# Top-32 attention and gated FFN on one core: the 64-row tiles of two head pairs worked as one couple, with three q, k and v buffers

## The chip, the core and the metric

The kernel runs on one core of a Trainium2 chip. The metric is the device time of one launch in microseconds (us). All operands are float32 in HBM. TensorE is called PE here, VectorE DVE, ScalarE ACT, GpSimd POOL and the engine that issues all loads and stores SP.

## The reference, cut to what matters

```python
def _attn_ref(q, k, v):                      # each (8, 8, 576, 64)
    scores = matmul(q, k.transpose(0, 1, 3, 2)) / sqrt(64)
    kth = np.partition(scores, -32, axis=-1)[..., -32:-31]
    scores = np.where(scores >= kth, scores, -1e9)
    attn = exp(scores - max(scores))
    attn = attn / (sum(attn) + 1e-09)
    return matmul(attn, v)

def _moe_ref(x, w_in, conv_w, w_out):        # x (8, 576, 512), d_ff 1024, 3 taps
    h = np.maximum(x @ w_in, 0.0)
    conv_out = sum over k of conv_w[k] * h shifted by k - 1 along the sequence
    return (h * sigmoid(conv_out)) @ w_out
```

## The kernel before, in words

Heads are worked in pairs: 8 batches of 4 pairs, and a pair's two heads lie on the two halves of the 128 partitions of q and k. The 576 query rows are four blocks of 128 and one of 64. A batch is worked in two parts (`PARTS`): part 0 has blocks 0 to 2 of all four pairs, part 1 has block 3 and the block of 64 rows (`None`). One tile of work is 128 partitions of 576 scores. A block of 128 rows gives two tiles, one per head (`t.h` 0 and 1). The block of 64 rows gives one tile, a *single*, with head 1 on the lower 64 partitions and head 0 on the upper. A batch so has 24 tiles in part 0 and 12 in part 1, in all 288. In part 1 the order is head 0, head 1, single, for each pair in turn.

A function `iteration(it)` writes out, tile by tile, what PE, DVE, ACT and POOL do in a fixed order. Several tiles are in flight: the tile that gets its scores in an iteration is 7 ahead of the one that DVE weighs, and that is one ahead of the one that PE transposes. The steps:

- `fetch` (L210) loads k (704 columns, 352 KB) and q (576 columns, 288 KB) of a pair on SP, one piece ahead; `nat` has two buffers (`NATB`). `load_v` (L215) loads v, in the iteration in which the pair's first tile reaches the stage `tC`.
- `edge_product` (L221) and `scores` (L227) fill the PSUM banks `s_ps[0]`, `s_ps[1]` and the 128 columns `edge_ps`, with the last 64 key columns of both heads. For a block of 128 rows both heads' scores are made at once, at `t.h == 0` (L242); a single has two products of 64 rows by 64 columns of the array (L235) for 512 keys and two for 64 keys.
- `evacuate` (L244, ACT) copies the scores to SBUF; DVE finds candidates for the 32nd largest (L266, L286, L288); ACT makes the signs (L300); POOL multiplies (L305); DVE takes a maximum (L315) and selects the threshold (`select`, L319); ACT makes the exponentials (`expo`, L312) into one PSUM buffer; DVE masks, weighs and sums (`weigh`, L333).
- `transposes` (L338, PE) and `transposed` (ACT) turn the weights; `tails` (L355, PE) and `tailed` (L360, ACT) do so for the last 64 columns. For a single, `tailed` is two copies of 64 by 64 (L367). `av` (L369, PE) multiplies with v; `av_out` (L383, ACT) copies the result out.
- An iteration is `crowded` (L795) when it makes the scores of an ordinary block; an `av` that would fall in a crowded iteration is put off to the next one.
- Between these PE works off pieces of the FFN (`Expand` L454, `Contract` L611), so many per iteration as a written budget gives: `FEED` 1.65 in part 0, `LEAN` 1.3 in part 1. Their other steps are on ACT (relu L468, tanh L515), POOL and DVE (gate L523).
- `inverses` (DVE) and `norms` (PE, ACT, then SP: one store of the sums and eight or more loads that spread them, `rb`) follow when two pairs are done.
- In the first iterations the weights, which come as float64, are converted, block by block (`Convert`, DVE L163, L164 and L175, ACT L168 to L172, POOL).
- After the last tile a loop works off what is left of the FFN. That loop stands outside the written order, and a planner may place its work earlier.

## Time and profile before

| | us |
|---|---|
| time before, median of 3 runs | 1126.01 (1123.76 to 1126.7) |
| the profiled execution | 1126.22 |
| its span | 1124.3 |
| busy PE / DVE / ACT / POOL | 1041.0 / 1044.5 / 985.1 / 959.8 |
| mean granted PE clock, share of full | 0.986 |

The profile shows one execution. Busy is the time in which an engine had an instruction running; PE's ends are modelled, and a busy PE is not always PE at its peak. Idle time of an engine is put down to what released it.

### The profile page before, as it was taken

The page shows a single profiled execution, that of the slowest core. Times are in us where ns is not written, and L with a number is a line of the kernel's source. Part 1 is how long each engine was busy: PE and PEld are TensorE (multiplying, and loading weights), DVE is VectorE, ACT ScalarE, POOL GpSimd, SP SyncE. Part 2 cuts the span into 40 slices and gives each one's busy share as a digit, 9 for nine tenths or more (in the row PEclk, how much of TensorE's full clock was granted, in tenths as well). Part 3 has the DMA queues.
Part 4 walks back from the last instruction along what each step waited for, and adds up shares of the span by engine and source line. Part 5 has one row for each costly group of instructions (what it writes and reads, how often), then busy time and mean ns, then how long its engine had stood idle before and what let it go on. Part 6 is the DMA issues. An engine that isn't in the chain of part 4 may idle for free.

```text
span 1124.3 us, 28000 instructions
## 1 busy us (share of the span) xinstructions
PE 1041.0 (93%) x7970; PEld 766.5 (68%) x7970; DVE 1044.5 (93%) x5822; ACT 985.1 (88%) x2504; POOL 959.8 (85%) x1260
## 2 busy tenths in 40 slices
PE   6765589999999999999999999999999999999997
PEld 1443356676777777776777777776777777776885
DVE  6999999999999999999999999999999999999760
ACT  6999989999899998989989898989989898989641
POOL 5989979799898989899898999899898999899800
PEclk9989889999999999999999999999999999999999
DMA  7232231123221331223221321223221331222101
GB/s 254 89 101 79 68 100 56 61 75 115 74 78 51 119 100 54 71 74 123 73 71 60 119 99 54 70 74 126 70 74 60 115 97 60 69 72 82 27 27 44
DMA packets 71157, 92.28 MB, mean 82 GB/s; under 512 B 12848, under 2 KB 37712, under 8 KB 70992
## 3 DMA queue, kind: packets, MB, share of 16 engines
q1 hardware_dynamic: 70992, 90.38, 25.1%
q8 instruction: 66, 1.08, 0.4%
q14 instruction: 99, 0.81, 0.2%
HBM read 80.76 MB, written 9.58 MB: 80 GB/s over the span
## 4 chain that ended last, share of the span: by engine, by line
PE 72%; DVE 17%; ACT 8%; issue 1%; DMA 1%; SPq 0%; ACTq 0%
PE mc L611 15%; PE me L454 14%; PE pt L345 11%; PE mixed L377 11%; PE s L242 9%; DVE cand L266 4%; DVE e L333 3%; DVE z L315 3%; PE mixed L380 2%; PE s L235 2%; PE mixed L225 2%; ACT weights_ps L312 2%; PE mixed L358 2%; PE weights_ps L611 1%; ACT side L300 1%
## 5 line engine op out<-in xcount | busy, mean ns | idle before, releaser
L266 DVE MAX8 cand<-rows 128x8 f32<-128x82 f32 (+1 forms) x2016 | 483.9, 242 | 0.0
L305 POOL TENSOR_TENSOR z<-rows,side 128x579 f32<-128x579 f32 x288 | 347.3, 1206 | 58.5 <-ACT side L300 56.2
L333 DVE SCALAR_TENSOR_TENSOR e<-rows,kth,weights_ps 128x576 f32<-128x576 f32 x288 | 232.2, 806 | 1.5 <-PE mixed L358 0.9
L454 PE MATMUL me<-x_hi,wi 128*128 128x258 f32 (+1 forms) x952 | 229.9, 312 | 1.0 <-ACT g L468 1.0
L312 ACT ACTIVATE weights_ps<-rows,z 128x576 f32<-128x576 f32 x288 | 219.9, 764 | 6.1 <-DVE e L333 4.4
L300 ACT ACTIVATE side<-rows 128x576 bf16<-128x576 f32 x288 | 222.9, 774 | 0.0
L315 DVE MAX8 z<-z 128x8 f32<-128x576 f32 x288 | 214.3, 744 | 1.8 <-POOL z L305 1.8
L345 PEld LDWEIGHTS pt<-ident,e 128*128 128x128 f32 x1152 | 124.5, 144 | 121.5 <-issue 47.6
L611 PE MATMUL mc<-wo,split 128*128 128x512 f32 x732 | 197.1, 402 | 0.0
L353 ACT COPY pT<-pt 128x512 f32<-128x512 f32 x256 | 152.5, 596 | 49.0 <-PE pt L345 48.0
L345 PE MATMUL pt<-ident,e 128*128 128x128 f32 x1152 | 193.6, 292 | 0.2 <-DVE e L333 0.2
L242 PE MATMUL s<-k,q 64*128 64x512 f32 x512 | 178.3, 671 | 3.7 <-ACT rows L248 3.6
L248 ACT COPY rows<-s 128x512 f32<-128x512 f32 x288 | 166.6, 578 | 16.2 <-PE s L242 13.2
L377 PE MATMUL mixed<-pT,vn 128*64 128x128 f32 (+1 forms) x2560 | 166.1, 273 | 2.1 <-ACT pTt L363 2.1
L454 PEld LDWEIGHTS me<-x_hi,wi 128*128 128x128 f32 x952 | 162.9, 191 | 1.7 <-ACT g L468 1.7
L377 PEld LDWEIGHTS mixed<-pT,vn 128*64 128x64 f32 x2560 | 130.7, 139 | 24.1 <-issue 7.2
L611 PEld LDWEIGHTS mc<-wo,split 128*128 128x128 f32 x732 | 128.9, 189 | 20.5 <-issue 0.2
L454 PE MATMUL me<-x_lo,wi 128*128 128x258 f32 (+1 forms) x476 | 142.0, 298 | 0.0
L487 POOL TENSOR_SCALAR t<-g,cr 128x256 f32<-128x256 f32 (+1 forms) x230 | 117.4, 511 | 0.0
L286 DVE MAX8 rows<-cand 128x8 f32<-128x21 f32 x576 | 107.0, 186 | 0.0
L501 POOL TENSOR_TENSOR t<-t,t 128x256 f32<-128x256 f32 (+1 forms) x115 | 92.3, 803 | 9.6
L454 PEld LDWEIGHTS me<-x_lo,wi 128*128 128x128 f32 x476 | 91.1, 191 | 0.0
(133 smaller groups left out, 1788.0 us busy)
## 6 DMA issues: line engine op xcount, KB each, us to landing
k<-in_k_dram SPq DMA_DIRECT2D x64, 352.0 KB
q<-in_q_dram SPq DMA_DIRECT2D x64, 288.0 KB
vn<-in_v_main_dram SPq DMA_DIRECT2D x64, 256.0 KB
out_dram<-o SPq DMA_DIRECT2D x26, 256.0 KB
rb<-row SPq DMA_DIRECT2D x64, 96.0 KB
raw<-in_w_in_dram SPq DMA_DIRECT2D x16, 256.0 KB
vt<-in_v_tail_dram SPq DMA_DIRECT2D x64, 64.0 KB
raw<-in_w_out_dram SPq DMA_DIRECT2D x16, 256.0 KB
```

What stands on the lines that cost most here:

```text
L242: nc.tensor.matmul(s_ps[h], lhsT=qx[d, at], rhs=kx[d, h * TAIL:h * TAIL + MAIN], start=True, stop=True)
L248: nc.scalar.copy(out=x[:, at:at + MAIN], in_=s_ps[t.h])
L266: yield lambda c=c, at=at, n=n: nc.vector.max(out=t.cand[:, c:8 * CHUNKS:CHUNKS], in_=t.x[:, at:at + n])
L300: nc.scalar.activation(out=t.side[:, 2:S + 2], in_=t.x, func=AF.Sign, scale=-OVER, bias=t.row[:, 7:8], accum_out=t.cnt)
L305: nc.gpsimd.tensor_tensor(t.z[:, 8:S + 11], t.row[:, 6:S + 9], t.side, ALU.mult)
L312: nc.scalar.activation(out=e_ps, in_=t.x, func=AF.Exp, scale=scale, bias=t.shift)
L315: nc.vector.max(out=t.z[:, 0:8], in_=t.z[:, 10:S + 10])
L333: nc.vector.scalar_tensor_tensor(out=t.e, in0=t.x, scalar=kth[:, t.n:t.n + 1], in1=e_ps, op0=ALU.is_ge, op1=ALU.mult, accum_out=t.pc.sums[ ...
L345: nc.tensor.transpose(tp[:, i * P:(i + 1) * P], t.e[:, o + i * P:o + (i + 1) * P], ident)
L377: nc.tensor.matmul(a[r, 0:w], lhsT=st.pc.vn[:, h, i], rhs=st.pT[:, 1 - h if st.single else h, i, 0:w], start=(i == 0), stop=False)
L454: nc.tensor.matmul(mm[:, 0:w], lhsT=wt, rhs=xx, start=(n == 0), stop=(n == len(ops) - 1))
L611: nc.tensor.matmul(mm[0:m], lhsT=x[:, i], rhs=wo[:, e, f], start=start, stop=stop)
```

## The change

The blocks of 64 rows of two pairs (an even one and the odd one after it) become one *couple* of two tiles, which is treated like an ordinary block of two tiles: the even pair's 64-row block is tile `t.h == 0` and goes to bank `s_ps[0]`, the odd pair's is `t.h == 1` and goes to `s_ps[1]`. In the even pair's tile head 1 is on the lower partitions, in the odd pair's tile head 0 is. The number of tiles stays 288. In part 1 the order becomes two tiles of the even pair, two of the odd pair, two of the couple, so all iterations alternate between crowded and not.

Per couple: four products of 64 by 64 quarters of the array for 512 keys, and two products of the whole array for 64 keys each, from padded operands that the host lays out (`last` behind q, `both` behind k); one evacuation of 128 edge columns at `t.h == 0`; one tail transposition; four tail copies of 64 by 64; the `av` of both pairs one after another, from one weights tile. `fetch` loads only the q columns that the part needs (384 or 320 instead of 576; k 704 or 768), into three buffers; it may run six tiles ahead. `load_v` is three stages later (`tE`), with three buffers. At the start one pair is fetched ahead of the first weights, not two.

```diff
-NATB = 2
+NATB = 3
+VB = 3
+AHEAD = 6
...
     def fetch(pc):
-        for nm, src in (("k", k), ("q", q)):
-            x = pc.nat[nm] = nat.tile([P, src.shape[3]], F32, name=nm, bufs=NATB)
-            nc.sync.dma_start(out=x, in_=src[pc.b, pc.g])
+        last = None in PARTS[pc.part]
+        for nm, src, a, z, w in (("k", k, 0, S + 3 * TAIL if last else S + 2 * TAIL, S + 3 * TAIL),
+                                 ("q", q, pc.c0, S + P if last else pc.c1, WIDE)):
+            x = pc.nat[nm] = nat.tile([P, w], F32, name=nm, bufs=NATB)
+            nc.sync.dma_start(out=x[:, 0:z - a], in_=src[pc.b, pc.g, :, a:z])
...
     def edge_product(t):
         t.edged = True
-        row = row_of(t.st.i)
-        at = slice(row, row + P)
-        nc.tensor.matmul(edge_ps, lhsT=t.pc.nat["q"][:, at], rhs=t.pc.nat["k"][:, S:S + 2 * TAIL], start=True, stop=True)
+        if t.single:
+            for one in (t, t.mate):
+                nc.tensor.matmul(edge_ps[:, one.h * TAIL:(one.h + 1) * TAIL],
+                                 lhsT=one.pc.nat["q"][:, one.st.c + TAIL:one.st.c + TAIL + P],
+                                 rhs=one.pc.nat["k"][:, S + 2 * TAIL:S + 3 * TAIL], start=True, stop=True)
...
     def scores(t):
...
+        for one in (t, t.mate) if t.single else (t,):
+            kx, qx, at = one.pc.nat["k"], one.pc.nat["q"], one.st.c
+            for h in range(2):
+                d, keys = slice(h * D, (h + 1) * D), slice(h * TAIL, h * TAIL + MAIN)
+                if t.single:
+                    r = slice(half_of(one, h) * D, (half_of(one, h) + 1) * D)
+                    nc.tensor.matmul(s_ps[one.h][r], lhsT=qx[d, at:at + TAIL], rhs=kx[d, keys], start=True, stop=True)
...
     def evacuate(t):
...
-        if t.single:
-            nc.scalar.copy(out=x[:, MAIN:S], in_=edge_ps[:, 0:TAIL])
-        elif t.h == 0:
+        if t.h == 0:
...
     def tailed(t):
...
+        for one in (t.mate, t):
+            c = slice(one.h * TAIL, (one.h + 1) * TAIL)
             for h in range(2):
-                r = slice(h * TAIL, (h + 1) * TAIL)
-                nc.scalar.copy(out=pTt[r, 0:TAIL], in_=t.tp[0:TAIL, (1 - h) * TAIL:(2 - h) * TAIL])
+                at = half_of(one, h) * TAIL
+                nc.scalar.copy(out=pTt[h * TAIL:(h + 1) * TAIL, c], in_=tail_ps[c, at:at + TAIL])
...
-        crowded = n < NT and not work[n].single and work[n].h == 0
+        crowded = n < NT and work[n].h == 0
...
-            if t.k == 0 and n and pcs.index(pc) + 1 < len(pcs):
-                fetch(pcs[pcs.index(pc) + 1])
+            tiles[n] = work[n]
+            while state.fetched < len(pcs) and n >= pcs[state.fetched].first - AHEAD and (
+                    state.fetched < NATB or n > pcs[state.fetched - NATB].scored):
+                fetch(pcs[state.fetched])
+                state.fetched += 1
...
-        if tC is not None and tC.k == 0:
-            load_v(tC.pc)
+        if tE is not None and tE.k == 0:
+            load_v(tE.pc)
...
             if both:
                 tail_next.append(tE)
-                tE.st.at = it + 1
-                av_next.append(tE.st)
+                for st in tE.unit.sts:
+                    st.at = it + 1
+                    av_next.append(st)
...
-        for pc in pcs[0:2]:
-            fetch(pc)
+        fetch(pcs[0])
+        state.fetched = 1
         load_blocks(W_FIRST)
```

## Rows read from the trace of the kernel before

**Rows 1.** The page: busy us of each engine, share of the span, instructions.

```profile
PE 1041.0 (93%) x7970; PEld 766.5 (68%) x7970; DVE 1044.5 (93%) x5822; ACT 985.1 (88%) x2504; POOL 959.8 (85%) x1260
```

**Rows 2.** One line, the weighing on DVE: min/median/max ns, first and last start.

```profile
L333 DVE SCALAR_TENSOR_TENSOR e<-rows,kth,weights_ps x288: 792/806/817, 27.9 to 1051.7; 128x576 f32<-128x576 f32 x144
```

**Rows 3.** Windows, parts 0 and 1 of batches 3, 4: length, engines, PE clock, DMA.

```profile
422.18:507.65 85.47, 85.15 (x658) 64.55 (x658) 81.56 (x470) 77.04 (x194) 78.43 (x104) 1.00 0.23 72
507.65:549.90 42.25, 38.36 (x341) 27.77 (x340) 41.24 (x239) 39.51 (x103) 37.62 (x49) 1.00 0.34 106
549.90:632.79 82.89, 82.69 (x646) 63.32 (x645) 81.25 (x470) 76.73 (x194) 76.23 (x99) 1.00 0.22 70
632.79:675.46 42.67, 41.18 (x356) 30.40 (x353) 41.39 (x239) 39.18 (x103) 39.84 (x50) 1.00 0.33 106
```

**Rows 4.** Timeline of DVE: start, us, instruction, idle time before it and releaser.

```profile
137.55 0.23 DVE L319 SCALAR_TENSOR_TENSOR hot<-weights_ps,cnt,z 128x10 f32<-128x10 f32 x1 [0.26 <-ACT weights_ps L312]
...
429.29 0.23 DVE L319 SCALAR_TENSOR_TENSOR hot<-weights_ps,cnt,z 128x10 f32<-128x10 f32 x1 [0.69 <-ACT weights_ps L312]
...
1051.33 0.23 DVE L319 SCALAR_TENSOR_TENSOR hot<-weights_ps,cnt,z 128x10 f32<-128x10 f32 x1 [2.08 <-ACT weights_ps L312]
```

**Rows 5.** Timeline of ACT ahead of the wait that ends at 429.29.

```profile
427.43 0.59 ACT L353 COPY pT<-pt 128x512 f32<-128x512 f32 x1 [0.67 <-PE pt L345]
427.91 0.42 ACT L367 COPY pTt<-mixed 64x64 f32<-64x64 f32 x2
428.34 0.27 ACT L387 COPY xt<-mixed 128x128 f32<-128x128 f32 x1
428.50 0.75 ACT L312 ACTIVATE weights_ps<-rows,z 128x576 f32<-128x576 f32 x1
```

**Rows 6.** Timeline of PE: scores of a single, then of an ordinary block.

```profile
503.13 1.08 PE L235 MATMUL s<-k,q 64*64 64x512 f32 x4
...
504.04 0.28 PE L235 MATMUL mixed<-k,q 64*64 64x64 f32 x4
...
506.89 1.13 PE L242 MATMUL s<-k,q 64*128 64x512 f32 x4
```

**Rows 7.** One group by form: shapes, count, busy us, mean ns, idle before.

```profile
L358 PE MATMUL mixed<-ident,e 128*64 128x128 f32 x32 | 9.2, 287 | 12.2 <-ACT pTt L363 8.3 <-ACT xt L387 4.0
```

**Rows 8.** Timeline of PE: products with v of a block, then of a single.

```profile
417.48 1.09 PE L377 MATMUL mixed<-pT,vn 128*64 128x128 f32 x16
418.40 0.39 PE L380 MATMUL mixed<-pTt,vt 128*64 128x128 f32 x4
418.62 0.63 PE L377 MATMUL mixed<-pT,vn 128*64 128x64 f32 x16
419.08 0.29 PE L380 MATMUL mixed<-pTt,vt 128*64 128x64 f32 x4
```

**Rows 9.** Timeline of the start: SP, PE, DVE and ACT, with idle times.

```profile
1.65 0.43 SPq L213 DMA_DIRECT2D k<-in_k_dram  x1
...
2.60 0.43 SPq L153 DMA_DIRECT2D raw<-in_conv_w_dram  x1
...
4.68 0.77 PE L225 MATMUL mixed<-k,q 128*128 128x128 f32 x2 [4.68 <-DMA q<-in_q_dram]
7.67 0.19 DVE L163 TENSOR_SCALAR mc<-raw 128x24 uint32<-128x24 uint32 x1 [5.60 <-DMA raw<-in_conv_w_dram]
...
8.84 0.58 ACT L248 COPY rows<-s 128x512 f32<-128x512 f32 x1
```

**Rows 10.** Timeline of SP: the last of eight spreading loads, and a load of v.

```profile
409.82 0.61 SPq L414 DMA_DIRECT2D rb<-row  x1
411.37 0.35 SPq L218 DMA_DIRECT2D vn<-in_v_main_dram  x1
```

**Rows 11.** Windows behind that load of v: the last two columns are DMA share and GB/s.

```profile
414.00:415.00 1.00, 1.00 (x6) 0.30 (x4) 1.00 (x11) 0.37 (x2) 0.92 (x3) 1.00 0.00 0
```

**Rows 12.** The chain that ended last, in order of time, at the end.

```profile
1110.59 5.48 PE weights_ps L611 x24
```

More of the change, by code (lines that the diff above doesn't have):

```diff
@@ L73, in attend_and_feed @@
     v_main, v_tail = v
-    B, NPAIR, _, S = q.shape
+    (B, NPAIR), S = q.shape[:2], out.shape[1]
     D = P // 2
@@ new lines, in scores @@
+    def scores(t):
+        if t.h:
+            return
+        if not t.edged:
+            edge_product(t)
+        for one in (t, t.mate) if t.single else (t,):
[5 more added lines that the diff above has]
+                    nc.tensor.matmul(s_ps[one.h][r], lhsT=qx[d, at:at + TAIL], rhs=kx[d, keys], start=True, stop=True)
+                else:
+                    nc.tensor.matmul(s_ps[h], lhsT=qx[d, at:at + P], rhs=kx[d, keys], start=True, stop=True)
@@ L681, in attend_and_feed, with add_unit @@
     pcs, work = [], []
+    def add_unit(sts):
+        unit, pair = Box(), []
+        for h in range(2):
+            st = sts[h % len(sts)]
+            t = Box()
+            t.n, t.k, t.h, t.pc, t.st, t.single, t.unit = len(work), st.pc.n, h, st.pc, st, len(sts) > 1, unit
+            t.edged = False
+            st.pc.n += 1
+            st.pc.scored = len(work) - h
+            work.append(t)
+            pair.append(t)
+        unit.sts = sts
+        pair[0].mate, pair[1].mate = pair[1], pair[0]
+        for h, st in enumerate(sts):
+            st.unit, st.off = unit, h * TAIL
+            st.half = [half_of(pair[h], i) for i in range(2)] if len(sts) > 1 else range(2)
     for b in range(B):
@@ L685, in attend_and_feed @@
                 pc = Box()
[L686 to L689 removed]
+                pc.b, pc.g, pc.part, pc.nat, pc.n, pc.sts = b, g, part, {}, 0, []
+                pc.c0 = pc.c1 = MAIN if blocks[0] is None else blocks[0] * P
                 for i in blocks:
                     st = Box()
[L692 to L701 removed]
+                    st.pc, st.c, st.w, st.final = pc, pc.c1 - pc.c0, TAIL if i is None else P, i == blocks[-1]
+                    pc.c1 += st.w
+                    pc.sts.append(st)
+                pcs.append(pc)
+                pc.first = len(work)
+                for st in pc.sts:
+                    if st.w == P:
+                        add_unit([st])
+                if g % 2 and None in blocks:
+                    add_unit([x.sts[blocks.index(None)] for x in pcs[-2:]])
     NT = len(work)
@@ L794, in iteration @@
             pass
-        crowded = n < NT and not work[n].single and work[n].h == 0
+        crowded = n < NT and work[n].h == 0
         avs = [st for st in av_next if not crowded or it > st.at]
         av_next = [st for st in av_next if st not in avs]
-        both = tE is not None and tE.ends
+        both = tE is not None and tE.h == 1
         if tE is not None:
@@ L873, in iteration @@
         while recs and not crowded:
-            norms(recs.pop(0), s_ps[1 if n < NT and work[n].single else 0])
+            norms(recs.pop(0), s_ps[0])
         rec_next = recs + rec_next
@@ L877, in iteration @@
             tails(tE)
-        if n + 1 < NT and not (work[n].single or work[n + 1].single or work[n + 1].h):
+        if n + 1 < NT and not work[n + 1].h:
             edge_product(work[n + 1])
@@ L933 @@
     nc = tc.nc
-    B, NPAIR, _, S = q.shape
+    (B, NPAIR), S = q.shape[:2], out.shape[1]
     DM, DF = w_in.shape
@@ L1001, in _layout @@
     ends = ends.reshape(B, H // 2, 2 * D, -1)
+    both = np.concatenate([k[:, h::2, main:].transpose(0, 1, 3, 2) for h in range(2)], axis=2)
+    last = np.zeros((B, H // 2, 2, D, 2, S - main), q.dtype)
+    for h in range(2):
+        for g in range(H // 2):
+            last[:, g, h, :, h if g % 2 else 1 - h] = q[:, 2 * g + h, main:].transpose(0, 2, 1)
+    last = last.reshape(B, H // 2, 2 * D, -1)
     tails = np.zeros((B, H // 2, 2, S - main, 2, D), v.dtype)
@@ L1006, in _layout @@
     arrays = {
-        "q": pairs(q, lambda h: False),
-        "k": np.concatenate([pairs(k, lambda h: h % 2 == 1), ends], axis=-1),
+        "q": np.concatenate([pairs(q, lambda h: False), last], axis=-1),
+        "k": np.concatenate([pairs(k, lambda h: h % 2 == 1), ends, both], axis=-1),
         "v_main": v[:, :, :main].reshape(B, H // 2, 2, main // P, P, D).transpose(0, 1, 4, 2, 3, 5),
```

80 lines of the change are left out of this document (25 added, 55 removed).

## The prediction

> **What bounds the kernel now.** I read the page first, then the weighing line, then windows, then the timelines around single waits. The page says little by itself: PE and DVE are both busy for 93% of the span [rows 1]. The weighing line gives the clockwork: 288 weighings from 27.9 to 1051.7 us, 3.57 us apart on average [rows 2]. So the span is a start of 28 us, 1024 us of tiles, and 72 us in which the rest of the FFN is worked off.
>
> Cut at the weighings, the windows show who fills the tile phase [rows 3]. In part 1 DVE is busy for 41.24 of 42.25 us (batch 3) and 41.39 of 42.67 (batch 4), while PE is at 38.36 and 41.18. In part 0 PE is busy for nearly all of it (85.15 of 85.47, 82.69 of 82.89) and DVE for 81.56 and 81.25. So DVE's work, which the change leaves as it is, is a floor. In part 1 only about 1 us in 42 lies above it, and the part in which PE is full is the one whose work does not change. That is the main argument against a large gain.
>
> What lies above the floor are short waits on DVE. Its timeline shows waits whose line is mostly the selection L319, released by ACT [rows 4]. Sorted by the tile that is weighed next, 29 of them, 16.4 us, fall in part 1 or on the first four tiles after one (the first, at 137.55 us, and the last, 2.08 us at 1051.33, are shown). Six of these, 4.4 us, are in the last part 1, where the pipeline drains; the other 23 hold 12.0 us. From batch 1 on another 26 waits, 11.5 us, lie deep in part 0 and stay. One wait shows the mechanism: ahead of 429.29 ACT had waited 0.67 us for PE's transpositions, then made the two tail copies of a single, 0.42 us, a copy of 0.27 us, and only then the exponentials for which DVE stood 0.69 us [rows 4, 5]. PE's lateness and ACT's copies add up.
>
> **The change, part by part.** The sum is made against the profiled execution, 1126.22 us (span 1124.3 and 1.9 around it), which is 0.2 us above the median of 1126.01.
>
> *The start.* Today conv_w is queued behind two pairs' k and q, 2 x (352 + 288) = 1280 KB; then behind one pair's, 352 + 192 = 544 KB. SP issues it two places earlier, 2.60 - 1.65 = 0.95 us, and 736 KB less lie ahead. Two loads of 640 KB each, issued from 0.74 and 1.65 us, have let the first q through at 4.68 and conv_w at 7.67 [rows 9], so about 640 KB cost at most 3 us. DVE waited 5.60 us for conv_w, and the first evacuation on ACT, at 8.84, stands behind its conversion. The scores are ready sooner than that, since PE begins them at 4.68 us. I take 1.5 us earlier, between 0 (a later weight block is what holds, for the second pair's loads now stand between the blocks) and 2.2 us.
>
> *PE's work.* Two singles cost 2 x (1.08 + 0.28) = 2.7 us of scores [rows 6]. A couple has four products for 512 keys. If all four quarters run together they cost what one single's two do, 1.08 us; if not, twice that, 2.16. The nearest rows speak for the first: the two quarters of a single take 1.08 us and the two halves of an ordinary block, with twice the columns, 1.13 [rows 6], so products in separate parts of the array run side by side. I take 1.08. The two edge products I put at the 0.28 us of a single's four, the nearest row. Together 1.36, with one tail transposition of 0.29 us less [rows 7]: 1.6 us saved per couple (bounds 0.5 and 1.6), 16 couples, 26 us of PE (8 to 26). The products with v keep their number. Today a single's can fall into one iteration with an ordinary block's, 1.09 + 0.39 + 0.63 + 0.29 [rows 8]; then a couple's two fall together, 2 x (0.63 + 0.29) = 1.84, so the heaviest iteration gets 0.56 us lighter.
>
> A rule of the Trainium skill speaks against the side by side: TensorEngine Tiling (Array Packing), under Gotcha 1: PSUM Pressure, says that different row tiles cannot access the same PSUM bank simultaneously. A single's two products are in different row halves and write one bank, and their 1.08 us is no longer than the 1.13 us into two banks [rows 6], so here the trace differs from the rule. By the rule a couple's scores would take the 2.16 us, and the time would be that of the third rival.
>
> *What PE's saving is worth.* Only waits above the floor can go: the 12.0 us, if each of them is PE's doing. In the wait that I traced, 0.67 us was PE's and 0.42 us the tail copies'. I take half, 6.0 us, bounds 0 and 12.0.
>
> *ACT's copies.* The couple makes four tail copies in one iteration where a single made two: 0.42 us more at a place where expo had no room left [rows 5]. In the sum over six tiles nothing is added, and one copy of 128 edge columns replaces two of 64. ACT has room on average (39.51 of 42.25 us [rows 3]), so only the bunching can cost: 16 x 0.42 = 6.7 us if all of it shows, 0 if PE's earliness covers it. I take half of it, 3.2 us.
>
> *Loads.* Less traffic, on nobody's path: the DMA share is 0.22 to 0.34 [rows 3], and after the first q no wait of PE names k, q or v. Three buffers let SP run ahead; nothing waits for that today, so 0. The later load of v costs cover: its lead falls from six iterations to three, 10.5 us. SP spends 8 x 0.61 = 4.9 us on eight spreading loads that can stand ahead of such a load, and v itself, issued from 411.37, has landed by 414, since the queue then moves nothing [rows 10, 11]: 4.9 + 2.6 = 7.5 us, under the 10.5, so hidden by 3.0 us. Without that cover PE would stand in `av`, with its transpositions queued behind. In part 1 a fetch of k and q may now wait for the couple's scores; v and the sums are behind it on SP, with the same three iterations of lead. No new wait stands on DVE.
>
> *The end.* The last couple's products with v and copies come later by one single's, 0.92 + 0.42 us, but the chain from there to 1116 is PE on FFN products [rows 12], which fill that gap. I take 0; if the cover fails 1.3 us more, and if the drain's longest wait goes 2.1 us less [rows 4].
>
> Sum: -1.5 - 6.0 + 3.2 = -4.3, so 1126.2 - 4.3 = **1121.9 us**. With all good ends it would be 1109.9 (-2.2 - 12.0 - 2.1), with all bad ones 1134.2 (+6.7 + 1.3).
>
> **The rivals.**
>
> *Nothing but the start.* DVE's floor takes PE's saving and ACT's bunching is just covered: 1126.2 - 1.5 = 1124.7. For it: 97 to 98% busy DVE in part 1. Against: the waits at 429.29 and its like begin with PE.
>
> *All waits go.* PE's 1.6 us per couple keeps it ahead of ACT throughout, the copies are covered: 1126.2 - 1.5 - 12.0 - 2.1 = 1110.6. Against: half of a traced wait is not PE's.
>
> *The quarters don't run together*, so the change does not do what it says: 0.5 of 1.6 us is saved, 6.0 x 0.5 / 1.6 = 1.9 us of waits go, the copies cost their 3.2: 1126.2 - 1.5 - 1.9 + 3.2 = 1126.0.
>
> *ACT becomes the late one*, and the kernel slower. Place: the crowded iteration after a couple's transposition, where signs, evacuation, transposed copy, four tail copies and a result copy all stand ahead of expo. Price 0.42 us a couple, 6.7 in all, with no wait gone: 1126.2 - 1.5 + 6.7 = 1131.4. It decides from the point at which expo has under 0.42 us of room before the selection; at 429.29 it had none [rows 4, 5]. Against: PE's transpositions may come earlier. The Trainium skill says the like, in TensorEngine Tiling (Array Packing), PSUM Bottleneck: tiling speeds up TensorE but not PSUM evacuation, and the copy may become the bottleneck. No run here shows it yet.
>
> A late v would cost about 1 us at 16 ends of two pairs, some 1141; the 3.0 us of cover speak against it.
>
> **How the numbers follow.** About 0.3%, 3.4 us, can be told from no change here: faster means under 1122.8, slower over 1129.6. Chances: the forecast 0.40 (its own range 1118 to 1124, a quarter of it above 1122.8), only the start 0.22, all waits 0.11, quarters in turn 0.08, ACT late 0.16, v late 0.03. Faster: 0.30 + 0.11 + 0.04 = 0.45; slower 0.15 + 0.03 + 0.02 from the edges of others = 0.20; the same 0.35. The range reaches to all waits gone and to ACT late, 1111 to 1131.5, with half of each beyond it and v late: 0.16 left out.
>
> **What would show it.** Start: the first weighing at 26.4 instead of 27.9 us. Quarters: eight records in about 1.1 us for a couple; about 2.2 would prove the third rival. Waits: in part 1 and just behind it about 6 us of DVE's idle time fewer, and new ones of up to 0.4 us behind four tail copies. PE's busy time in a part 1 stretch falls by some 3 us while DVE's stays at 41.2 to 41.4. A PE wait that names v would show the load too late. The prediction is wrong if the part 0 stretches change by more than 1 us, for nothing in my sum acts there, or if the stretch after 1052 us differs by over 2 us, which the planner's freedom there allows.

## The result, and the profile of the changed kernel

The changed kernel takes 1114.69 us (median of 4 runs, 1114.14 to 1115.66), the kernel before 1125.43 in the same comparison. The ratio is 0.9906, with a 95% interval of 0.9889 to 0.9924: faster by 10.7 us where 4.3 were forecast. The direction was right and the time lies inside the range; the size is two and a half times the forecast.

The profiled execution of the changed kernel took 1114.14 us, with a span of 1112.0. Its page, busy us of each engine, share of the span and instructions, against [rows 1]:

```profile
PE 1023.4 (92%) x7890; PEld 760.7 (68%) x7890; DVE 1042.2 (94%) x5824; ACT 978.7 (88%) x2483; POOL 955.2 (86%) x1257
```

The weighing line, with min/median/max ns and the first and last start, against [rows 2]:

```profile
L337 DVE SCALAR_TENSOR_TENSOR e<-rows,kth,weights_ps x288: 791/803/816, 25.6 to 1042.0; 128x576 f32<-128x576 f32 x144
```

So the start became 2.4 us shorter (27.9 to 25.55), the tiles 7.3 us (1023.75 to 1016.45), and what follows the last weighing 2.6 us (72.6 to 70.0). The windows of parts 0 and 1 of batches 3 and 4, with the columns of [rows 3]:

```profile
416.78:501.67 84.89, 84.89 (x677) 65.33 (x676) 81.45 (x470) 76.67 (x196) 79.41 (x106) 1.00 0.23 70
501.67:543.11 41.44, 39.83 (x325) 29.13 (x323) 41.07 (x238) 38.24 (x99) 38.40 (x50) 1.00 0.30 93
543.11:626.38 83.27, 79.93 (x650) 60.75 (x649) 81.05 (x471) 77.28 (x196) 75.60 (x98) 1.00 0.21 68
626.38:668.15 41.77, 40.15 (x328) 29.46 (x326) 41.13 (x239) 38.14 (x98) 38.27 (x49) 1.00 0.30 92
```

Part 1 fell from 42.25 and 42.67 us to 41.44 and 41.77. Part 0 fell by 0.58 us in batch 3 and rose by 0.38 in batch 4. Over all batches part 0 gave 2.2 us, part 1 5.1; of the latter 1.5 are in batch 0 alone, a stretch that differs by as much between the variants of the changed kernel below that have three buffers (40.9 to 42.6 us). DVE's busy time fell as well, by 0.1 to 0.3 us a stretch in this table, though the same instructions ran.

What DVE waited for, us in total, times, longest:

```profile
DVE hot L323 <- ACT weights_ps L519: 16.3, 40, 0.7
DVE hot L323 <- ACT weights_ps L316: 7.2, 11, 2.7
```

By the tile that is weighed next, 12 waits of 7.9 us lie in part 1 or on the four tiles behind it (29 of 16.4 us before), and 40 of 15.9 us deep in part 0 (26 of 11.5 before). Many short ones, released by the tanh on ACT, have taken the place of fewer long ones. Six of the forty, of 0.73 or 0.74 us, stand ahead of the fifth tile of part 0 in batches 2 to 7, where none stood before; where they come from is read below, from the run with one copy.

On PE the change did what it says. A couple's edge products and its scores on PE's timeline, and then the groups that the change touches (busy us, mean ns | idle before):

```profile
490.14 0.56 PE L228 MATMUL mixed<-k,q 128*128 128x64 f32 x4
...
493.50 1.09 PE L246 MATMUL s<-k,q 64*64 64x512 f32 x8
```

```profile
L246 PE MATMUL s<-k,q 64*64 64x512 f32 x128 | 18.8, 639 | 0.0
L228 PE MATMUL mixed<-k,q 128*128 128x64 f32 x64 | 9.3, 270 | 0.0
L360 PE MATMUL mixed<-ident,e 128*128 128x128 f32 x144 | 42.7, 297 | 47.6 <-ACT rows L260 47.6
```

The same groups of the kernel before, the third being [rows 7] and the ordinary blocks' tails together:

```profile
L235 PE MATMUL s<-k,q 64*64 64x512 f32 x128 | 34.4, 615 | 1.0 <-ACT rT L400 1.0
L235 PE MATMUL mixed<-k,q 64*64 64x64 f32 x128 | 9.3, 223 | 2.8 <-ACT xt L387 2.8
L358 PE MATMUL mixed<-ident,e 128*128 128x128 f32 (+1 forms) x160 | 46.2, 289 | 43.6 <-ACT rows L256 19.9 <-ACT xt L387 14.8 <-ACT pTt L363 8.3
```

A couple's four products leave eight records and take 1.09 us: the four quarters run together. PE's busy time fell by 15.6 us in the scores, by nothing in the edge products, by 3.5 in the tail transpositions.

### The profile page after: what moved, and what is told of

It reads as the page before. It is cut to its first block, busy times and chain, and to the rows that moved or that the text cites. A ratio compares the mean times of both kernels' runs of the same rounds, so it can differ in the third digit from the quotient of the medians.

```text
span 1112.0 us, 27779 instructions
## 1 busy us (share of the span) xinstructions
PE 1023.4 (92%) x7890; PEld 760.7 (68%) x7890; DVE 1042.2 (94%) x5824; ACT 978.7 (88%) x2483; POOL 955.2 (86%) x1257
## 4 chain that ended last, share of the span: by engine, by line
PE 55%; DVE 31%; ACT 10%; DMA 1%; issue 1%; POOL 0%; SPq 0%; ACTq 0%; POOLq 0%
PE mc L615 13%; PE me L458 12%; PE pt L349 8%; DVE cand L270 8%; PE mixed L381 8%; DVE e L337 7%; PE s L248 7%; DVE z L319 5%; DVE cand L292 3%; ACT weights_ps L316 2%; DVE g L527 2%; DVE rows L290 2%; ACT side L304 2%; PE mixed L384 2%; PE weights_ps L615 1%; PE mixed L232 1%
## 5 line engine op out<-in xcount | busy, mean ns | idle before, releaser
L270 DVE MAX8 cand<-rows 128x8 f32<-128x82 f32 (+1 forms) x2016 | 482.2, 241 | 0.2 <-issue 0.2
L458 PE MATMUL me<-x_hi,wi 128*128 128x258 f32 (+1 forms) x952 | 227.4, 310 | 0.0
L248 PE MATMUL s<-k,q 64*128 64x512 f32 x512 | 172.5, 668 | 5.7 <-ACT rows L254 4.5
L381 PEld LDWEIGHTS mixed<-pT,vn 128*64 128x64 f32 x2560 | 132.7, 142 | 17.4 <-issue 1.1
```

The costliest lines, as they stand in the source:

```text
L248: nc.tensor.matmul(s_ps[h], lhsT=qx[d, at:at + P], rhs=kx[d, keys], start=True, stop=True)
L270: yield lambda c=c, at=at, n=n: nc.vector.max(out=t.cand[:, c:8 * CHUNKS:CHUNKS], in_=t.x[:, at:at + n])
L381: nc.tensor.matmul(a[r, 0:st.w], lhsT=st.pc.vn[:, h, i], rhs=st.unit.pT[:, st.half[h], i, c], start=(i == 0), stop=False)
L458: nc.tensor.matmul(mm[:, 0:w], lhsT=wt, rhs=xx, start=(n == 0), stop=(n == len(ops) - 1))
```

## The experiments

All twelve runs stand in one table, below the two kernels. Times are medians; the ratio is to the kernel before on the same chip. The last three columns are from the profiled execution: first weighing, time from first to last weighing, time behind the last.

| run | us | ratio, 95% interval | first | tiles | behind |
|---|---|---|---|---|---|
| before | 1125.43 | 1 | 27.92 | 1023.75 | 72.63 |
| changed | 1114.69 | 0.9906 (0.9889 to 0.9924) | 25.55 | 1016.45 | 70.00 |
| b_startnew | 1123.3 | 0.9984 (0.9974 to 0.9993) | 26.31 | 1025.07 | 71.82 |
| b_tailspace | 1194.16 | 1.061 (1.058 to 1.064) | 27.35 | 1092.38 | 71.67 |
| b_halfscores | 1122.37 | 0.9972 (0.9962 to 0.9982) | 28.14 | 1022.31 | 70.65 |
| a_startold | 1116.51 | 0.993 (0.9913 to 0.9947) | 28.24 | 1016.42 | 70.74 |
| a_scorestwice | 1119.85 | 0.995 (0.9933 to 0.9967) | 25.78 | 1022.91 | 70.91 |
| a_uncrowd | 1119.19 | 0.9954 (0.9937 to 0.997) | 25.62 | 1020.13 | 71.15 |
| a_secondfree | 1115.15 | 0.9915 (0.9893 to 0.9937) | 25.77 | 1016.24 | 70.99 |
| a_spread | 1118.56 | 0.9949 (0.993 to 0.9969) | 25.76 | 1019.18 | 70.96 |
| a_twotails | 1113.63 | 0.9901 (0.9885 to 0.9918) | 25.55 | 1015.93 | 71.22 |
| a_twobuf | 1133.83 | 1.0071 (1.0046 to 1.0097) | 25.31 | 1035.14 | 72.05 |
| a_onecopy | 1107.93 | 0.9845 (0.9829 to 0.9862) | 25.78 | 1010.54 | 70.78 |
| a_both | 1109.61 | 0.9861 (0.9844 to 0.9877) | 25.74 | 1006.94 | 75.82 |

Names with b_ are built on the kernel before, names with a_ on the changed one. A size against the changed kernel is the difference of two ratios times 1125 us. With intervals of about 0.0017 to each side such a difference is good to some 2.7 us; the stretches of the trace, which repeat from batch to batch, are much sharper, and I read those first.

**The start alone, on the kernel before.**

```diff
-            if t.k == 0 and n and pcs.index(pc) + 1 < len(pcs):
+            if t.k == 0 and pcs.index(pc) + 1 < len(pcs):
...
-        for pc in pcs[0:2]:
-            fetch(pc)
+        fetch(pcs[0])
```

> The kernel before with one edit: only the first pair's k and q are fetched ahead of the first weights, the second pair's one iteration later (with full q rows, two buffers, v as before). The changed kernel weighs its first tile at 25.55 us, the kernel before at 27.92. Theory: conv_w stood behind the second pair's 640 KB, and that alone is the start's gain: first weighing at 25.5 to 26.0 us, total lower by 2.0 to 2.4 us, tile stretch and end as before (1023.8 and 72.6 us). Rival: the smaller q slices or the later v make the start: first weighing within 1 us of 27.9. The tile stretch also tells whether VectorE's instructions, 0.3% shorter in the changed kernel's profile, differ from run to run: if they do, its busy time in the tiles differs from 992.2 us here too.

The weighing line begins at 26.3:

```profile
L333 DVE SCALAR_TENSOR_TENSOR e<-rows,kth,weights_ps x288: 792/806/818, 26.3 to 1051.4; 128x576 f32<-128x576 f32 x144
```

1.6 us earlier than before, and 1.8 us in the time (0.0016 of 1125). DVE's wait for conv_w is 3.8 us where [rows 9] have 5.60.

**The old start, on the changed kernel.**

```diff
-        fetch(pcs[0])
-        state.fetched = 1
+        for pc in pcs[0:2]:
+            fetch(pc)
+        state.fetched = 2
```

> The changed kernel with only its start put back: two pairs' k and q are fetched ahead of conv_w again, though with the new lengths (2 x 544 KB). If the start is a term of its own, the first weighing comes between 26.3 and 27.6 us (25.55 with one pair) and the time is 0.8 to 2 us longer than the changed kernel's 1114.7, that is 1115.5 to 1116.7; the tiles stay at 1016.5 us and the end at 70.0, within 1 us each. If the start also reaches into the tile phase (the rows of the first batch, 102.06 us), the first batch's part 0 moves by more than 1 us. The run is also the measure for how much DVE's instructions and the tile phase differ between two profiled executions: if its 2016 ranking instructions come out near 485 us where the changed kernel's were 482.2, then the 2.9 us by which DVE's busy time fell is a property of the execution and not of the change.

```profile
L337 DVE SCALAR_TENSOR_TENSOR e<-rows,kth,weights_ps x288: 792/806/819, 28.2 to 1044.7; 128x576 f32<-128x576 f32 x144
```

The first weighing comes at 28.24 us, later than the 26.3 to 27.6 that were expected: the start is 2.7 us longer, and the time by 2.7 (ratios). The stretches of batches 1 to 6 are those of the changed kernel to 0.02 us (part 0 of batch 3 is 84.88, part 1 41.45). The first batch differs, 142.7 us for both parts against 143.9. Its ranking instructions were recorded as 490.0 us in all where the changed kernel has 482.2, and the stretches didn't move: these durations overlap one another, so their sum can't be taken for time, and the lengths of the stretches have to be.

**PE's saving taken back: a couple's four products made twice.**

```diff
-        for one in (t, t.mate) if t.single else (t,):
+        for one in (t, t.mate, t, t.mate) if t.single else (t,):
```

> The changed kernel with the four score products of a couple made twice (8 more records, about 1.1 us of TensorE per couple, 17 us in all); the result is the same. Theory of the prediction: TensorE's saved time ends the waits in the tiles, so giving two thirds of it back returns 3 to 5 us of the tile stretch (1016.5 to about 1020), mostly in part 1 and the tiles behind it. Rival: the even rhythm (no iteration with two products with v on top of an ordinary block's, no tail right behind a tail) is what helps, and TensorE has room in part 1: the tile stretch grows by less than 1.5 us.

The group of the scores, and parts 0 and 1 of batch 3:

```profile
L246 PE MATMUL s<-k,q 64*64 64x512 f32 x256 | 33.3, 629 | 0.0
```

```profile
419.48:505.23 85.75, 85.75 (x685) 65.64 (x684) 81.58 (x471) 76.83 (x196) 80.20 (x107) 1.00 0.22 69
505.23:546.68 41.45, 40.41 (x333) 29.45 (x331) 41.07 (x238) 38.26 (x99) 37.66 (x48) 1.00 0.30 93
```

14.5 us of PE come back, 0.9 per couple, and the time is 5.0 us longer (ratios). Part 0 of each batch from 1 to 7 is 0.6 to 0.9 us longer, 5.8 us in all, also in the even ones; part 1 of batches 1 to 5 doesn't move (41.45 here, 41.44 in the changed kernel). The reason stands on the timeline above: the couple scored at 493.50 is scored in part 0, which ends at 501.67, since scores run seven tiles ahead of the weighing. The weighings show the place: in batches 2 to 4 the tiles run as in the changed kernel, to 0.03 us, up to the 23rd of part 0, and from the 24th on 0.85 us later, with no second step in part 1. This couple's saving is worth nearly all of itself; that of the second couple, scored in part 1, nothing. The size is what was expected, the place is not.

**PE's saving alone, in the old order.** Half of the scores of the singles are left out.

```diff
-            for to, n, ps_of in ((0, MAIN, s_ps[0]), (MAIN, TAIL, edge_ps)):
+            for to, n, ps_of in ((0, MAIN // 2, s_ps[0]), (MAIN, TAIL, edge_ps)):
```

> The kernel before with only half of a single's scores computed: each of its two products covers 256 keys instead of 512, so PE does about 0.5 us less per single, 1.0 us per two, in the iterations where the change saves PE's time; the order, the tail space, the iteration that counts as crowded and ACT's copies stay those of before. The ranking then works on old scores for the other half. If PE's saving by itself is what the change gained, at 1.0 of some 1.6 us per couple, the tiles fall from 1023.8 us by 3 to 6 us and the time goes to 1118 to 1121. If the gain needed the new rhythm and the freed tail space, little happens: 1122.5 to 1125, with the part 0 stretches at 85.5 and 82.9 and part 1 at 42.2 and 42.7 us as before.

The group of the scores, and parts 0 and 1 of batches 3 and 4:

```profile
L235 PE MATMUL s<-k,q 64*64 64x256 f32 x128 | 20.8, 402 | 1.0 <-ACT rT L400 1.0
```

```profile
422.73:507.76 85.03, 84.71 (x659) 64.65 (x660) 81.42 (x469) 77.15 (x195) 77.95 (x103) 1.00 0.23 72
507.76:549.16 41.40, 37.10 (x339) 27.66 (x340) 41.13 (x238) 38.94 (x103) 37.88 (x49) 1.00 0.35 108
549.16:632.06 82.90, 82.70 (x650) 63.56 (x649) 81.25 (x470) 76.98 (x194) 76.15 (x99) 1.00 0.22 71
632.06:676.24 44.18, 41.55 (x352) 31.25 (x351) 41.63 (x239) 38.48 (x102) 39.76 (x51) 0.96 0.31 101
```

13.6 us less of PE, much the same amount as in the run before, and 3.2 us in the time (0.0028 of 1125), between the two expectations. Batch 3 is 0.44 and 0.85 us shorter; batch 4's part 0 is as before and its part 1 is 1.5 us longer, and so is that of batch 1 (1.3). In batch 4 this is what PE did, and the granted clock (last column but two), around 656 us:

```profile
653.00:656.20 3.20, 1.55 (x11) 0.75 (x8) 3.20 (x21) 3.20 (x9) 3.12 (x4) 1.00 0.23 86
656.20:659.60 3.40, 3.40 (x27) 2.85 (x26) 3.40 (x20) 1.73 (x5) 3.20 (x6) 0.50 0.01 3
```

```profile
656.55 1.98 PE L377 MATMUL mixed<-pT,vn 128*64 128x128 f32 x16
```

PE had stood idle for half of the 3.2 us before, the clock fell from 2.4 to 1.2 GHz for 3.4 us, and products with v that take 1.09 us in [rows 8] took 1.98. The weighing that follows is 1.08 us late. The same is seen at 277.3 us in batch 1, with 1.07 us; the kernel before has no such drop in batches 1 to 6. Whether PE's shorter work brings the drops or chance does isn't shown. Without these two, the gain would be some 5.4 us instead of 3.2, an estimate from the two steps. So it isn't shown that this PE time is worth less in the old order than in the new, where it was worth 5.0 us, good to some 2.7.

**One part of the rhythm undone.** The iteration that scores a couple isn't crowded any more, so products with v that are due run in it.

```diff
-        crowded = n < NT and work[n].h == 0
+        crowded = n < NT and not work[n].single and work[n].h == 0
```

> The changed kernel with one part of its rhythm undone: the iteration that scores a couple counts as not crowded, as an iteration with a single did, so products with v and the sums' products that are due run in it and do not wait for the next one. PE's amount of work is the same. If the rhythm (products with v kept out of the iterations with scores) is where the gain beyond the forecast came from, 16 such iterations get heavier by 0.6 to 1.2 us on PE and the waits come back: part 0 (first couple of a batch) or part 1 (second) longer by 0.3 to 0.8 us each, 3 to 8 us in all, 1118 to 1122. If only PE's sum counts, the time stays within 1.5 us of 1114.7.

5.4 us longer (ratios); in the profiled execution the tiles are 3.7 us longer and what follows them 1.1. Part 0 is longer by 0.5 us in batches 3, 5 and 7 and by 1.1 to 1.4 in 1, 2, 4 and 6, part 1 of batches 1 to 6 shorter by 0.3 to 0.6. PE's timeline here, at the first couple of batch 3:

```profile
494.24 1.09 PE L246 MATMUL s<-k,q 64*64 64x512 f32 x8
495.26 1.09 PE L381 MATMUL mixed<-pT,vn 128*64 128x128 f32 x16
496.18 0.39 PE L384 MATMUL mixed<-pTt,vt 128*64 128x128 f32 x4
496.50 0.65 PE L349 MATMUL pt<-ident,e 128*128 128x128 f32 x4
```

and the same place in the changed kernel:

```profile
493.50 1.09 PE L246 MATMUL s<-k,q 64*64 64x512 f32 x8
494.52 0.66 PE L349 MATMUL pt<-ident,e 128*128 128x128 f32 x4
```

The transpositions come 2.26 us behind the scores instead of 1.02. ACT and then DVE of the run with the rhythm undone show what that starts:

```profile
496.67 0.27 ACT L260 COPY rows<-mixed 128x128 f32<-128x128 f32 x1 [0.54 <-PE mixed L384]
497.19 0.59 ACT L357 COPY pT<-pt 128x512 f32<-128x512 f32 x1 [0.26 <-PE pt L349]
...
497.83 0.77 ACT L316 ACTIVATE weights_ps<-rows,z 128x576 f32<-128x576 f32 x1
```

```profile
498.63 0.23 DVE L323 SCALAR_TENSOR_TENSOR hot<-weights_ps,cnt,z 128x10 f32<-128x10 f32 x1 [0.40 <-ACT weights_ps L316]
```

ACT's copy of the edge columns waits for the products with v, which write the same tensor (mixed), then its transposed copy waits for PE, and the selection stands 0.40 us for the exponentials behind them. The changed kernel has no wait at that tile.

**The same for the second couple of a batch alone.**

```diff
-        crowded = n < NT and work[n].h == 0
+        crowded = n < NT and work[n].h == 0 and not (work[n].single and work[n].pc.g == 2)
```

> The changed kernel with the rhythm undone for the second couple of a batch alone: it is scored while DVE is at the third tile or so of part 1. With it undone for both couples part 0 got 0.5 to 1.4 us longer and part 1 0.35 to 0.6 us shorter. If each couple acts where it is scored, part 1 of batches 1 to 6 is again 41.1 to 41.3 us (41.45 and 41.77 in the changed kernel) and part 0 stays at 83.3 and 84.9: 2 to 4 us less, 1111 to 1113. If the second couple's rhythm is what costs part 0 (its products with v fall to the first tiles of the next part 0), part 0 gets longer by 0.5 to 1.4 us and the time is 1116 to 1119.

Neither came: 1.0 us longer by the ratios, within their error, part 0 unchanged (84.88 and 83.28), part 1 0.12 us longer (41.57 and 41.89). So the rhythm counts for the first couple, which is scored in part 0, and both what it gives there and what it costs part 1 come from that one.

**Two buffers for q, k and v.**

```diff
-NATB = 3
-VB = 3
+NATB = 2
+VB = 2
```

> The changed kernel with two buffers each for q, k and v in place of three; the order of the work is the changed kernel's. If the third buffer is needed because a couple holds both pairs' k and q until it is scored, the fetch for the next pair waits for that, k and q land late, PE waits that name q or k appear in part 1 and after it, and the time goes up by 5 to 40 us. If two were enough, as the forecast has it by putting the buffers at nothing, the time stays within 1.5 us of 1114.7 and no wait of PE after the start names q, k or v.

18.6 us longer than the changed kernel, and 0.7% longer than the kernel before. PE's waits:

```profile
PE mixed L232 <- DMA q<-in_q_dram: 25.2, 15, 4.2
```

One of them, of 4.2 us, is the start's; the others, 21.0 us, lie behind it. A couple holds the k and q of both its pairs until it is scored, and with two buffers the next pair's fetch starts only then.

**ACT's copies: one for four.** The tail of the transposed probabilities is copied whole, and a second layout of v's tail rows, half of it zeros, takes the quarters apart.

```diff
-        for one in (t.mate, t):
-            c = slice(one.h * TAIL, (one.h + 1) * TAIL)
-            for h in range(2):
-                at = half_of(one, h) * TAIL
-                nc.scalar.copy(out=pTt[h * TAIL:(h + 1) * TAIL, c], in_=tail_ps[c, at:at + TAIL])
+        nc.scalar.copy(out=t.unit.pTt, in_=tail_ps)
...
```

> The changed kernel with one tail copy of 128 by 128 instead of four of 64 by 64 per couple; the products with v take their 64 rows from it through a second, padded form of the last rows of v (64 KB more per pair in part 1). ScalarE has about 0.55 us less in the crowded iteration behind a couple's tail. If the bunched copies cost what the prediction put (half of 0.42 us a couple), the time falls by 2 to 4 us, in part 1 and just behind it. If ScalarE has room there, it changes by less than 1 us.

6.9 us less than the changed kernel, where 2 to 4 or nothing were expected, and 17.4 (1.55%) less than the kernel before: this version beats both. Part 0 of batches 2 to 7 is 0.7 us shorter each, 4.4 in all, part 1 of batches 1 to 6 stays. The whole 0.7 us arises at one place, ahead of the fifth tile of part 0, but it is made earlier, in part 1. The first couple's copies on the changed kernel's ACT there, the copy of the edge columns behind them, and PE, which waits for that copy:

```profile
527.61 0.85 ACT L371 COPY pTt<-mixed 64x64 f32<-64x64 f32 x4
...
530.64 0.27 ACT L260 COPY rows<-mixed 128x128 f32<-128x128 f32 x1
```

```profile
530.96 0.33 PE L360 MATMUL mixed<-ident,e 128*128 128x128 f32 x1 [0.51 <-ACT rows L260]
```

With one copy PE doesn't wait at that place:

```profile
528.57 0.28 PE L362 MATMUL mixed<-ident,e 128*128 128x128 f32 x1
```

The weighings of the two runs lie 1.71 us apart here, PE from 531 us on 2.43: with four copies PE is 0.72 us later against DVE, and stays so for 25 us, also over the second couple's copies at 547.42, which add nothing. DVE has room for it in part 1; at the fifth tile of part 0 the room is gone:

```profile
556.46 0.23 DVE L323 SCALAR_TENSOR_TENSOR hot<-weights_ps,cnt,z 128x10 f32<-128x10 f32 x1 [0.74 <-ACT weights_ps L519]
```

The same tile with one copy, without a wait:

```profile
554.03 0.23 DVE L325 SCALAR_TENSOR_TENSOR hot<-weights_ps,cnt,z 128x10 f32<-128x10 f32 x1
```

PE reads as full in part 0 of batch 3 with one copy too, at 84.14 us of 84.14:

```profile
415.81:499.95 84.14, 84.14 (x672) 64.67 (x671) 81.42 (x470) 75.51 (x191) 79.04 (x105) 1.00 0.23 72
```

PE's work is the same in both. So a full PE in this column isn't by itself a floor: it can be working off a delay that it brought along from the stretch before.

**The four copies shared out over two iterations.**

```diff
-        for one in (t.mate, t):
+        if not t.todo:
+            t.todo = [t.mate, t]
+        some = [t.todo.pop(0)] if state.it + 3 < NT else t.todo
+        if some is not t.todo and t.todo:
+            tail_next.append(t)
+        for one in some:
...
```

> The changed kernel with the couple's four tail copies on ACT shared out over two iterations, two and two, as the two singles' were; their number and size are the same. Making one copy of the four gained 6.8 us. If it was the bunching of four in one iteration that cost, most of that is gained here too: 3 to 6 us, 1109 to 1112, in the part 0 stretches of batches 1 to 7 (about 0.5 us each). If it was their sum (0.84 against 0.27 us per couple), nothing is gained: 1113.5 to 1116, and the wait moves one tile on.

4.8 us longer than the changed kernel, where a gain or nothing was expected. Part 0 of batches 2 to 7 is 0.4 us longer. In batch 4 the wait of 0.74 us is still there (0.76), and a new one of 0.27 us has come a tile ahead of it. The tail space is also held one iteration longer, and PE waits for it:

```profile
PE mixed L360 <- ACT pTt L376: 9.1, 8, 2.1
```

**Two transpositions of half the columns, as the singles had them.** They go into one tail space, one after the other, and the copies fall two and two.

```diff
-        nc.tensor.transpose(tail_ps, t.unit.e2[:, MAIN:MAIN + P], ident)
+        at, n = (MAIN + t.h * TAIL, TAIL) if t.single else (MAIN, P)
+        nc.tensor.transpose(tail_ps[0:n], t.unit.e2[:, at:at + n], ident)
...
-        for one in (t.mate, t):
-            c = slice(one.h * TAIL, (one.h + 1) * TAIL)
-            for h in range(2):
-                at = half_of(one, h) * TAIL
-                nc.scalar.copy(out=pTt[h * TAIL:(h + 1) * TAIL, c], in_=tail_ps[c, at:at + TAIL])
+        c = slice(t.h * TAIL, (t.h + 1) * TAIL)
+        for h in range(2):
+            at = half_of(t, h) * TAIL
+            nc.scalar.copy(out=pTt[h * TAIL:(h + 1) * TAIL, c], in_=tail_ps[0:TAIL, at:at + TAIL])
```

> The changed kernel with the tails of a couple made as two singles' were: two transpositions of 64 columns in two iterations into the one tail space, so that the first waits for ACT's copy of the block before it and the second for the copies of the first; the copies on ACT fall two and two into two iterations, as in the run that shares them out. Against that run it differs by the waits for the tail space and 0.29 us of PE per couple. If the waits for the tail space were what held part 1 before (12.2 us of idle time ahead of this line, two waits of 1.79 us in the last part 1), part 1 goes back from 41.8 towards 42.3 us, 0.3 to 0.8 us each, and the end from 70.0 to 71 or more: 4 to 7 us over the run that shares the copies out. If they cost nothing, it is within 1.5 us of that run.

```profile
PE mixed L361 <- ACT pTt L371: 7.0, 14, 0.7
```

The waits for the tail space are back, nearly the 8.3 us of [rows 7], and the time is that of the changed kernel (0.6 us less, within the error): part 0 of batches 2 to 7 is 0.2 us longer and of batch 1 1.0, part 1 of batches 1 to 6 the same, the last part 1 2.4 us shorter and what follows it 1.2 longer. Neither expectation held against the run before: this one is 5.4 us faster than it. Together, the old waits for the tail space and the copies two and two cost next to nothing against one transposition and four copies; that a gain of the one hides a loss of the other isn't excluded, though sharing the copies out was no gain in the run before, which had waits for the tail space too.

**The tail space, on the kernel before.** The single's tail was given columns of its own in another bank.

```diff
-        t.tp = tail_ps
-        n = TAIL if t.single else P
-        nc.tensor.transpose(t.tp[0:n, 0:P], t.st.e2[:, MAIN:MAIN + n], ident)
+        if not t.single:
+            t.tp = tail_ps
+            nc.tensor.transpose(t.tp, t.st.e2[:, MAIN:MAIN + P], ident)
+            return
+        t.tp = weights_ps[:, S + 16 + SMAX:S + 16 + SMAX + TAIL]
+        for h in range(2):
+            r, o = slice(h * D, (h + 1) * D), slice((1 - h) * D, (2 - h) * D)
+            nc.tensor.matmul(t.tp[o], lhsT=t.st.e2[r, MAIN:MAIN + TAIL], rhs=ident[r, r], start=True, stop=True)
...
-                nc.scalar.copy(out=pTt[r, 0:TAIL], in_=t.tp[0:TAIL, (1 - h) * TAIL:(2 - h) * TAIL])
+                nc.scalar.copy(out=pTt[r, 0:TAIL], in_=t.tp[r])
```

> The kernel before with one edit: a single's last 64 columns are turned into their own 64 free columns of PSUM (as two products with the identity, from quarter to quarter), so that TensorE needn't wait until ScalarE has copied the block's tail out of the one tail space. Theory: that wait (12.2 us idle ahead of the 32 single tails in the rows of before, two of 1.79 us each on the last path) is what the couple took away beside the scores, and it makes the end: last weighing to end 70.0 to 71.0 us instead of 72.6, tiles 0 to 3 us shorter, total 2 to 5 us lower. Rival: the end is shorter because the planner placed the FFN work otherwise, or because the couple's scores are cheaper: the end stays at 72 to 73 us.

68.7 us slower (0.061 of 1125), and it says nothing of the tail space, because the new place brought a wait of its own. What DVE waits for:

```profile
DVE hot L319 <- ACT pTt L372: 89.3, 31, 4.5
```

The selection reads other columns of that same tensor, and now stands behind ACT's tail copies.

**One copy, and FFN work moved from part 0 to part 1.** The run with one copy, with two numbers of the planner changed.

```diff
-FEED = 1.65
-LEAN = 1.3
+FEED = 1.55
+LEAN = 1.5
```

> The changed kernel with one tail copy for a couple (1107.9 us) and the planner's share of FFN work moved: 1.55 instead of 1.65 us an iteration in part 0, 1.5 instead of 1.3 in part 1, the same sum over 36 tiles. With one copy PE is still busy for all of the odd batches' part 0 (84.15 us, DVE 81.4) and has 1.6 us to spare in part 1. If PE is what keeps part 0 above DVE's 81.4 us, 24 x 0.1 = 2.4 us of its work leave it and part 0 of batches 2 to 7 gets 0.5 to 1.5 us shorter, part 1 stays under 41.9 us, and the time is 1101 to 1106. If what is left is ACT's chain to the selection, the stretches stay within 0.3 us and the time within 1.5 us of 1107.9; if part 1 was full already, it gets 0.5 us longer in each and the time is 1109 or more.

The tiles get another 3.6 us shorter than with one copy, and the end gives back 5.0 (70.78 to 75.82). Parts 0 and 1 of batch 3, against 84.14 and 41.45 with one copy:

```profile
415.55:498.38 82.83, 82.77 (x662) 63.48 (x660) 80.83 (x469) 74.34 (x188) 77.91 (x104) 1.00 0.24 73
498.38:540.92 42.54, 40.13 (x330) 29.35 (x328) 41.53 (x239) 39.83 (x100) 38.38 (x50) 1.00 0.31 94
```

Here part 0 loses 1.3 us and part 1 gains 1.1. Over all batches part 0 loses 8.0 us and part 1 gains 4.4, so with less of PE's work part 0 does get shorter; but work that is pushed back lands behind the last tile, and the 1101 to 1106 us that were expected for this case did not come. The time is 1.8 us above that of one copy alone, within the error: no gain.

## Why the prediction was right in direction and short in size

*The start: right, and mis-sized.* Forecast -1.5 us with an end of -2.2; it was -2.4 in the traces. The wait for conv_w is 2.5 us, from 5.60 in [rows 9], and most of that reached the first weighing; the forecast took too little of it. The old start put back costs 2.7 us, the new start alone gives 1.6. Runs with the same start differ by up to 0.8 us in the first weighing (25.31 to 25.78 in the changed order, 27.35 to 28.14 in the old one), so whether anything else in the change acts here stays open. The shorter loads don't show: with them and the old start the first weighing is at 28.24.

*PE's work: the mechanism right, the size a little less.* The scores cost 1.09 us as forecast. The rule of the Trainium skill that spoke against it, in TensorEngine Tiling (Array Packing), Gotcha 1: PSUM Pressure, that different row tiles cannot access one PSUM bank simultaneously, differs from this trace too: of a couple's four products two, from two row halves, write each bank, and the four take 1.09 us where a single's two take 1.08. The edge products take 0.56 us where 0.28 were put, since the nearest row was of quarters and the new ones are of full width. So 19.1 us were saved, 1.2 per couple, not 1.6.

*What PE's saving is worth: the step that failed.* The forecast held that part 0 is the part "whose work does not change", and sorted DVE's waits by the tile that is weighed. PE works seven tiles ahead. Its own rows showed it: the single scored at 503.13 [rows 6] is scored in the part 0 that ends at 507.65 [rows 3]. With a couple's products made twice the cost came almost wholly in part 0, at 0.6 to 0.9 us per 0.9 of PE. PE's busy time in part 1, which was to fall by some 3 us, rose from 38.36 to 39.83 us in batch 3 and fell from 41.18 to 40.15 in batch 4; in batch 4's part 0 it fell from 82.69 to 79.93. Part 0, which was not to change by more than 1 us, did so only in batch 1, by 1.1 us; in the other stretches changes of both signs kept it small. The size of the term, 6.0 us, is near the 5.0 that 14.5 of the 19.1 us of PE are worth, but it was worked out from waits in part 1: that it came near is luck.

*The rhythm: priced at nothing, worth about 5 us.* The forecast noted that the heaviest iteration gets lighter and put no term to it. Keeping products with v out of the iteration that scores the first couple saves 1.24 us between the scores and the transpositions, and through ACT a wait on DVE. Of the 6.4 us by which the forecast fell short this is the largest term; next come the 3.2 us put on the copies, which no run shows as a cost of the change, and 0.9 us at the start. The three parts undone one at a time, 5.0 + 5.4 + 2.7, come to 13.1 us, against 10.7 for all, each good to some 2.7. So they can make up the whole of the gain; whether and how much they overlap is within the error.

*Waits in part 1.* 29 waits of 16.4 us became 12 of 7.9, 8.5 us less where the forecast had 6.0 less and some new ones. But new ones deep in part 0 made up 4.4 us, which no term had there: as much as the six waits at the fifth tile, which go with one copy.

*ACT's copies: a cost, but not shown to be one of bunching.* Forecast +3.2 for four copies in one iteration. The mechanism, copies that make exponentials late and DVE wait, is there: against one copy the four cost 6.9 us, 4.4 of it in the six waits at the fifth tile. But their sum was the same before, 0.42 us per single [rows 5], and two and two is no faster in either of the runs that tried it. Both of these brought waits for the tail space too, so whether the change made the copies dearer at all stays open. The Trainium skill's PSUM Bottleneck (TensorEngine Tiling (Array Packing)), which the forecast put beside the rival of a late ACT, advises one access to PSUM for several tiles; that is what gave the 6.9 us, though these copies take transposed weights out of PSUM and not the scores that were tiled. As a rival, ACT late with a slower kernel did not come.

*The tail space.* In [rows 7] stand 12.2 us of idle PE ahead of the singles' tails, and the forecast read only the duration in that row. Put back on the changed kernel, together with copies two and two, those waits cost nothing that shows in the time, and 0.2 us in part 0 of each of batches 2 to 7; on the kernel before they couldn't be taken away by themselves.

*Loads: the zero was right, for a reason that needs the third buffer.* "Nothing waits for that today" is true, but without it PE waits 21.0 us for q behind the start. It isn't room to spare; it is what the couple needs. No wait of PE names v, so the later load was hidden as worked out.

*The end.* Forecast 0, measured -2.6 us in one pair of traces. Behind the last weighing the four kernels in the old order lie between 70.65 and 72.63 us, and the changed one's variants, the last run and the one with two buffers apart, between 70.0 and 71.2. So at most about 1 us is the change's, and what makes it stays open.

## What to carry to other kernels

In a software pipeline, sort the work of an engine by when that engine does it, not by the tile that another engine has in hand: here seven tiles lay between, and they moved half of the saving into the stretch that was thought untouched. A full PE was no floor, since it can carry a delay along from a stretch in which it stood idle; DVE's busy time held as one: no stretch of batches 1 to 6 fell more than 0.3 us below what it was before. PE and ACT release each other, so 0.58 us of copies on ACT in part 1 and 0.9 us of products on PE in part 0 both came out as time in part 0, 0.7 and 0.85 us. Price the order as well as the amounts: the iteration in which a product runs was worth about as much as the products saved.

## What the runs showed of the hardware that was not expected

Four products in the four quarters of the array, two row halves writing each of two banks, take 1.09 us where two in two quarters took 1.08. When PE had stood idle for half of 3.2 us, its granted clock was 0.50 for the next 3.4 us in the run with half of the scores, and products with v took 1.98 us for 1.09. A copy of 128x128 took 0.27 us on ACT, and four of 64x64 took 0.85, though together they move as much. And in this program waits went by whole tensors in PSUM: ACT's copy of the edge columns stood 0.54 us for products with v in other columns of the same one, and the selection 89.3 us for tail copies that were put beside what it reads.
